# Retention, routed attention and a token mixer on one core: retention outputs ahead of the next scores, weights ahead of the third chunk, token tiles between transposes and outputs of the last batch

## The chip, the cores and the metric

The kernel runs on one core of a Trainium2 chip. Five engines run their own instruction streams and meet at semaphores: TensorE (PE; its weight loads are listed as PEld), VectorE (DVE), ScalarE (ACT), GpSimd (POOL) and SyncE (SP), which here only issues DMAs. The metric is the device time of one execution in microseconds (us). The kernel before takes 981.37 us as the median of 3 runs (979.86 to 984.8).

## The reference, cut to what matters

Three blocks follow each other on 8 batches of 576 positions.

```python
# 1 retention, 8 heads of 64
scores = q @ k.T / 8 ;  x = (scores * gamma_h ** (i - j) * (i >= j)) @ v
# 2 four softmax heads, of which a gate keeps two per position
for e in range(4):
    a = softmax(causal((x @ wq[e]) @ (x @ wk[e]).T / 8))
    out += gate[:, :, e] * (a @ (x @ wv[e]) @ wo[e])
# 3 token mixer on x = out
theta = x @ w_theta
y = w_tok_r @ (x * cos(theta)) + w_tok_i @ (x * sin(theta))
u = x + y ;  out = u + max(u @ w_ch, 0)
```

The weights of block 3 arrive as 64-bit floats, and the kernel itself converts them to pairs of 32-bit numbers.

## The kernel before, in words

The positions of a batch are cut into five chunks of 128 (the last has 64). Numbers are kept as a rounded high part and a rest, so most products are three matmuls (`mm3`, L94 to L96: high by high, low by high, high by low).

**Retention** of a batch is five chunks. `ret_scores` (L132) makes the scores of a chunk in two PSUM tiles named `w`; DVE masks them into `sm` (L137, L140). `ret_out` carries the state in PSUM (`pS`, L153; ACT copies it, L155), makes the output in a third `w` tile (L160 state by queries, L164 `sm` by values), and DVE scales it (`xt`, L171). `ret_step(b, c)` does the scores of chunk c, then the output of chunk c-1. There are three buffers `w`, and they go round: retention, projections (`proj_qk` makes U or KN from x, L94 to L96; `proj_v` makes V and the gate's logits, L225) and later the token tiles take them in turn, so a tile waits until the one three places before it has been read.

**Attention** is 80 units (batch b, head pair p, row tile m), ten per batch. In step t the loop makes the scores of unit t in PSUM tiles `a` (L286; DVE takes the row minimum, L289; ACT the exponential, L294), does what the table `SLOTS` puts there ("Q01 K10" are projections, "R2" is a retention step, capitals of this batch, small letters of the next), transposes the unit before (L333; the copies out of PSUM to `PT` are L338 and L340, one head on DVE, one on ACT), and where a group of row tiles is full makes its outputs (L352, copied by ACT at L356). So retention of batch b+1 and its projections run inside the steps of batch b. PE executes in the order in which this loop is written; the other engines' orders and SP's are made by the framework's scheduler.

**Converting** the weights of block 3 is 53 jobs, dealt out over the steps by `JOBS`: 40 up to step 63, 13 up to step 81. A job is a DMA (`raw`, L413), five DVE operations (L420 to L426), two of ACT and three of POOL, and a DMA back to DRAM.

**The last batch** (steps 70 to 80) has no retention. At step 69 `fuse_load` fetches w_theta and wo; at steps 72 and 73 `fuse` multiplies them (24 matmuls of 512 columns in all). At step 73 `load_o` fetches the attention outputs `ol` and the gates `og` of batches 0 and 1 and POOL multiplies them (L496). `EARLY_AT` sets nine `token_tile`s (1, 1, 2, 2, 1, 2 in steps 75 to 80) behind each step's outputs: 12 matmuls each, six into a `w` tile (x) and six into the single `pS` (theta); ACT copies x (L520), DVE reduces the angle (`k`, L523; `nr`, L525). After the loop `z_tile` (sine and cosine, L606 to L611, then a split to `zh` and `zl`, L99 and L100) feeds `mix` (L665), and `channel` ends the batch.

**The start** (`for c in range(NCH + 1)`): retention of batch 0, with the splits of the four weight tiles `wst` into WH and WL (L99, L100) and the first projections between the chunks. The DMA order there is: chunks 0 and 1, `g0`, one weight tile, chunk 2, three weight tiles.

Of the kernel before, what the change touches and what calls it, by code (L numbers as in the profile page):

```python
# [22 lines left out]
NCH = 5  # L23
# [24 lines left out]
WB = 3  # L48
JOBS = (63, 81)

EARLY_AT = {-5: 1, -4: 1, -3: 2, -2: 2, -1: 1, 0: 2}
EARLY = sum(EARLY_AT.values())

# [4 lines left out]
def tile_kernel(ctx: ExitStack, tc: tile.TileContext, qk, kv, w1, wo, wot, wd, cst, out):  # L58
# [11 lines left out]
    GD = [dram.tile([2, 2, 640], F32, name=f"gd{b}") for b in range(B)]  # L70
    att = pool("att", side="right")
    w1p = pool("w1p", side="right")
    ret = pool("ret", side="right")
# [104 lines left out]

    def ret_step(b, c):
        if c < NCH:  # L180
            ret_scores(b, c)
        if c:
            ret_out(b, c - 1)

# [3 lines left out]
    def proj_qk(b, p, t, g):  # L188
        xh, xl = XT[b]
        if (b, p) not in QKP:  # L190
            QKP[b, p] = (att.tile([128, 2, S], F32R, name="U", bufs=2), att.tile([128, 2, 2, S], F32R, name="KK", bufs=2),
                         att.tile([128, 2, S], F32R, name="KN", bufs=2))
        U, KK, KN = QKP[b, p]
# [62 lines left out]
    def work(b, names):  # L256
        for n in names.split():
            x = b + n.islower()
            if x < B:
                if n in "Gg":  # L260
                    gate(x)
                elif n[0] in "Vv":
# [122 lines left out]
    nc.sync.dma_start(g0, cst[:, o + 1088 + E * E:].rearrange("p (a t) -> p a t", a=4))  # L385
    for c in range(NCH):
# [102 lines left out]
    def load_o(b):  # L489
        OL[b] = wk1.tile([128, 2, S], F32, name="ol", bufs=3)  # L490
        nc.sync.dma_start(OL[b], OD[b])
        gw = wk1.tile([128, 2, S], F32, name="og", bufs=1)
        for s in range(2):
            for p in range(2):
                nc.sync.dma_start(gw[s * 64:s * 64 + 64, p, :], GD[b][p, s, :S].partition_broadcast(64))
        nc.gpsimd.tensor_mul(OL[b], OL[b], gw)  # L496

    def token_tile(pp, g, i):
# [27 lines left out]
        X2[g, i], NR[g, i] = x2, nr  # L526

    units = [(b, p, m) for b in range(B) for p in range(2) for m in range(NCH)]
    nu = len(units)
# [6 lines left out]
    due = [(JOBS[0] - 2) / njobs[0], (JOBS[1] - JOBS[0]) / njobs[1]]  # L536
    early = 0
    outs = []
    for t in range(nu + 1):
        b, k = divmod(t, 10)  # L540
        more, after = SLOTS[k] if t < nu else ("", "")
        if t < nu:
            at_scores(units[t])
            work(b, more)
            if units[t][2] == NCH - 1:
                at_norm(*units[t][:2])
        if t:
# [18 lines left out]
        if t == nu - 11:  # L566
            assert not jobs[0]
            ret.release()
            w2 = pool("w2")
            WOH, WOL, MH, ML = [w2.tile([128, 2, DM], F32R, name=x) for x in ("WOH", "WOL", "MH", "ML")]  # L570
            wa = pool("wa")
            fuse_load()
        if t in (nu - 8, nu - 7):
            fuse(t - nu + 8)
        if t == nu - 7:
            w1p.release()
            wa.release()
            w2b = pool("w2b")
            TK = w2b.tile([128, 9, 2, S], F32R, name="TK")
            wk1 = pool("wk1")  # L580
            load_o(0)
            load_o(1)
            for kt in KORD:
                nc.sync.dma_start(TK[:, kt].bitcast(F32), TD[kt])
        for _ in range(EARLY_AT.get(t - nu, 0)):
            token_tile(ps1, 0, early)
            early += 1
    assert not jobs[1]
# [9 lines left out]
    ps2 = pool("ps2", space=PSUM)  # L598
    ZT = {}

    def z_tile(g, i, h):

        x2, nr = X2[g, i], NR[g, i]
        ds = slice(h * 256, h * 256 + 256)
        cs = wk.tile([128, 2, 256], F32, name="cs", bufs=2)
        nc.vector.tensor_scalar(cs[:, 0, :].bitcast(I32), nr[:, ds].bitcast(I32), 0x7FFFFFFF, None, op0=OP.bitwise_and)  # L606
        nc.vector.tensor_scalar(cs[:, 0, :], cs[:, 0, :], math.pi / 2.0, None, op0=OP.subtract)  # L607
        nc.vector.tensor_scalar(cs[:, 1, :], nr[:, ds], PI_LO, -PI_LO, op0=OP.min, op1=OP.max)
        nc.scalar.activation(cs, cs, AF.Sin)  # L609
        z = cs  # L610
        nc.vector.scalar_tensor_tensor(z, cs, -1.0, x2[:, None, ds].to_broadcast([128, 2, 256]), op0=OP.mult, op1=OP.mult)  # L611
        if i != 4:
            zh = wk.tile([128, 2, 256], F32R, name="zh", bufs=4)
            zl = wk.tile([128, 2, 256], F32R, name="zl", bufs=4)
            split(zh, zl, z)
            ZT[g, i, h] = (zh, zl)
            return
        ZT[g, i, h] = []
        for b in range(2):
            zh = wk.tile([128, 256], F32R, name="zth", bufs=4)  # L620
            zl = wk.tile([128, 256], F32R, name="ztl", bufs=4)
            for a in range(2):
                split(zh[a * 64:a * 64 + 64], zl[a * 64:a * 64 + 64], z[b * 64:b * 64 + 64, a, :])
            ZT[g, i, h].append((zh, zl))

    UT = {}
# [72 lines left out]

    for i in range(early, 5):  # L700
        token_tile(ps2, 0, i)
    for b in range(B):
        q = [x for x in nxt_tiles(b) if x[0] or x[1] >= early]
        if b % 2 and b + 1 < B:
# [10 lines left out]
    ps2.release()  # L715
    wk.release()
    wk1.release()
    w2b.release()
    w2.release()
    cvt.release()  # L720
# [78 lines left out]
```

## Time and profile before

| | us |
|---|---|
| median of 3 runs | 981.37 |
| the profiled execution, its own time | 983.44 |
| its span, first to last instruction | 981.7 |
| PE busy in the span | 930.5 |
| DVE busy | 648.9 |
| ACT busy | 442.7 |
| POOL busy | 244.3 |

The span is what the rows below divide up; the execution's own time is 1.74 us longer, and it lies 2.07 us above the median. "Idle before" and what ended it is given in square brackets in a timeline. The granted clock of PE stands as a share of full speed: 1.00 is 2.4 GHz, 0.50 is 1.2 GHz, and values between are a mean over a stretch.

### The profile page before, as it was taken

The numbers are of one execution on the slowest core, as the hardware profiler recorded it, in microseconds if no ns is written. First come the engines' busy times: TensorE is split into PE (matmuls) and PEld (weight loads), VectorE is DVE, ScalarE is ACT, GpSimd is POOL, SyncE is SP. The second block draws the span as 40 slices with busy tenths as digits, with TensorE's granted clock in tenths as the row PEclk, the third lists the DMA queues.
The fourth block names the chain that finished last, engine by engine and source line by source line (L and its number), as shares of the span: only waits on it lengthen the run. The fifth ranks groups of instructions, "written<-read, shape, count | busy, mean of one in ns | idle before, by whom it ended". The sixth has DMA issues, their size and how long they took to land.

```text
span 981.7 us, 21532 instructions
## 1 busy us (share of the span) xinstructions
PE 930.5 (95%) x8090; PEld 854.7 (87%) x8090; DVE 648.9 (66%) x1843; ACT 442.7 (45%) x1198; POOL 244.3 (25%) x290
## 2 busy tenths in 40 slices
PE   6999999999999899998977799999999999999998
PEld 5989888888898889887755799999999999999998
DVE  4477767768776787776557974495656846486533
ACT  2355546555564565555544533333343432344320
POOL 4324243342524334142214111021201102020110
PEclk9999999999999999999989999999999999999999
DMA  9856647556666566636755300021101001010001
GB/s 265 227 144 204 177 156 191 172 170 191 189 181 192 149 185 211 158 108 178 219 223 166 133 24 26 26 73 49 49 2 37 37 1 49 1 49 2 25 26 49
DMA packets 81016, 115.69 MB, mean 118 GB/s; under 512 B 17680, under 2 KB 55952, under 8 KB 80912
## 3 DMA queue, kind: packets, MB, share of 16 engines
q1 hardware_dynamic: 80768, 114.03, 39.0%
q8 instruction: 64, 1.05, 0.5%
q0 software_dynamic: 144, 0.28, 0.1%
q14 instruction: 40, 0.33, 0.1%
HBM read 71.94 MB, written 23.74 MB: 97 GB/s over the span
## 4 chain that ended last, share of the span: by engine, by line
PE 72%; DVE 12%; DMA 5%; ACT 5%; issue 2%; SPq 2%; POOL 1%; ACTq 0%; DVEq 0%; POOLq 0%
PE acc L665 22%; PE w L94 8%; PE w L95 8%; PE w L96 8%; PE a L286 4%; PE w L225 4%; PE a L352 4%; PE w L132 3%; PE w L164 3%; PE a L333 2%; PE w L160 2%; DMA raw<-wd 2%; DVE P L289 2%; PE acc L655 2%; DVE U L211 2%
## 5 line engine op out<-in xcount | busy, mean ns | idle before, releaser
L665 PE MATMUL acc<-TK,zh 128*128 128x256 f32 (+1 forms) x1024 | 185.0, 303 | 3.9 <-ACT zh L99 3.9
L665 PEld LDWEIGHTS acc<-TK,zh 128*128 128x128 f32 x1024 | 153.4, 191 | 4.8 <-ACT zh L99 4.3
L294 ACT ACTIVATE P<-P,st 128x128 f32<-128x128 f32 (+4 forms) x160 | 95.5, 598 | 55.6 <-DVE st L289 54.9
L665 PE MATMUL acc<-TK,zl 128*128 128x256 f32 (+1 forms) x512 | 110.8, 298 | 0.0
L691 POOL TENSOR_TENSOR o<-o,ul 128x576 f32<-128x576 f32 x28 | 42.5, 1522 | 229.8 <-DVE o L686 186.6
L289 DVE CUSTOM_DVE_ANT_0 P<-a,cm 128x128 f32<-128x128 f32 (+4 forms) x160 | 72.1, 478 | 27.7 <-PE a L286 27.4
L665 PEld LDWEIGHTS acc<-TK,zl 128*128 128x128 f32 x512 | 86.8, 190 | 0.1
L609 ACT ACTIVATE cs<-cs 128x512 f32<-128x512 f32 x72 | 45.3, 630 | 90.4 <-DVE cs L607 86.3
L611 DVE SCALAR_TENSOR_TENSOR cs<-cs,x 128x512 f32<-128x512 f32 x72 | 61.3, 856 | 26.7 <-ACT cs L609 26.3
L286 PE MATMUL a<-KK,U 128*64 128x288 f32 (+4 forms) x384 | 77.1, 329 | 1.3 <-issue 0.9
L94 PE MATMUL w<-uh,CH 128*128 128x256 f32 (+1 forms) x256 | 76.0, 298 | 2.4 <-DVE nr L525 1.3
L94 PE MATMUL w<-xh,WH 128*128 128x288 f32 x256 | 76.3, 298 | 0.0
L99 ACT ACTIVATE zh<-cs 128x512 fp32r<-128x512 f32 x64 | 40.2, 629 | 80.0 <-PE acc L665 61.1
L96 PE MATMUL w<-xh,WL 128*128 128x288 f32 x256 | 76.0, 297 | 0.0
L95 PE MATMUL w<-xl,WH 128*128 128x288 f32 x256 | 75.9, 296 | 0.0
L95 PE MATMUL w<-ul,CH 128*128 128x256 f32 (+1 forms) x256 | 75.7, 296 | 0.0
L100 DVE TENSOR_TENSOR zl<-cs,zh 128x512 fp32r<-128x512 f32 x64 | 45.2, 710 | 46.2 <-ACT zh L99 45.4
L96 PE MATMUL w<-uh,CH 128*128 128x256 f32 (+1 forms) x256 | 75.7, 296 | 0.0
L429 POOL TENSOR_TENSOR r<-r,ex 128x192 f32<-128x192 f32 (+1 forms) x51 | 29.3, 575 | 185.4 <-ACT hl L430 93.6
L352 PE MATMUL a<-PT,V 128*64 128x192 f32 (+3 forms) x576 | 57.1, 320 | 11.4 <-DVE PT L338 7.7
L286 PEld LDWEIGHTS a<-KK,U 128*128 128x128 f32 (+1 forms) x384 | 53.7, 172 | 12.5 <-issue 5.6
L100 DVE TENSOR_TENSOR ul<-acc,uh 128x256 fp32r<-128x256 f32 x64 | 25.7, 451 | 58.4 <-ACT uh L99 58.1
(141 smaller groups left out, 2266.3 us busy)
## 6 DMA issues: line engine op xcount, KB each, us to landing
kv<-kv SPq DMA_DIRECT2D x40, 512.0 KB
KK<-KN SPq DMA_DIRECT2D x128, 144.0 KB
raw<-wd SPq DMA_DIRECT2D x43, 192.0 KB
qz<-qk SPq DMA_DIRECT2D x64, 128.0 KB
kt<-qk SPq DMA_DIRECT2D x32, 256.0 KB
out<-o SPq DMA_DIRECT2D x28, 288.0 KB
td<-hl SPq DMA_DIRECT2D x27, 192.0 KB
TK<-td SPq DMA_DIRECT2D x9, 576.0 KB
```

The source lines that it names most:

```text
L94: nc.tensor.matmul(ps, ah, bh, start=first, stop=False)
L95: nc.tensor.matmul(ps, ah, bl, start=False, stop=False)
L96: nc.tensor.matmul(ps, al, bh, start=False, stop=last)
L100: nc.vector.tensor_sub(l, src, h)
L286: nc.tensor.matmul(ps[s][:R], U[:, s, rs], KK[:, s, x, j0:j1], start=x == 0, stop=x == 1)
L289: MARK["dve"] = nc.vector.tensor_tensor_reduce(Ps[s][:R, j0:j1], ps[s][:R], cm[:R, o + j0:o + j1], 1.0, st[:R, 0, s:s + 1] if i else 3.0e3 ...
L294: MARK["act"] = nc.scalar.activation(Ps[s][:R, :n], Ps[s][:R, :n], AF.Exp, bias=st[:R, last, s:s + 1], scale=-1.0, accum_out=SUM[p][:R, m, ...
L352: nc.tensor.matmul(po[s * 64:s * 64 + 64, c0:], V[:ROWS[j], j, 2 * p + s, :], v, start=j == 0, stop=j == last, skip_group_check=True)
L609: nc.scalar.activation(cs, cs, AF.Sin)
L611: nc.vector.scalar_tensor_tensor(z, cs, -1.0, x2[:, None, ds].to_broadcast([128, 2, 256]), op0=OP.mult, op1=OP.mult)
L665: nc.tensor.matmul(acc[d][j], A[:, dc], TK[:, kt, W, t0:t1], start=q == 0 and n == 0, stop=q == 8 and n == 2)
L691: nc.gpsimd.tensor_add(o, o, ul[:, et, :].bitcast(F32))
```

## The change

Four edits. First, `ret_step` makes the output of chunk c-1 before the scores of chunk c. Second, the four weight tiles are fetched ahead of chunk 2 of batch 0, and the start is written out: scores 0 and 1, output 0, output 1, two V projections, and then scores and output of chunks 2, 3 and 4 directly behind each other; the scale `gt` is made chunk by chunk. Third, a table `LAST` replaces `SLOTS` and `EARLY_AT` in the last batch: each step has work before the transposes, between transposes and outputs, and after; the two `fuse` products and the nine token tiles ("T") stand there, theta of every second tile goes to a `w` buffer, `load_o` of batches 0 and 1 moves from step 73 to 69, and the first two z tiles are made before the loop's buffers are given back (their pool `zp` takes the place of U, KK and KN, which have a pool of their own now). Fourth, `JOBS` is (58, 75): conversions end six steps earlier.

```diff
-JOBS = (63, 81)
-EARLY_AT = {-5: 1, -4: 1, -3: 2, -2: 2, -1: 1, 0: 2}
+JOBS = (58, 75)
+EARLY = 9
+LAST = [("Q01", "K10", ""), ("K11", "", ""), ("Q10", "F0", ""), ("Q11", "F1", ""), ("", "T", ""),
+        ("T", "T", ""), ("T", "", ""), ("T", "", ""), ("T", "T", ""), ("", "T", ""), ("", "T", "")]
...
     def ret_step(b, c):
+        if c:
+            ret_out(b, c - 1)
         if c < NCH:
             ret_scores(b, c)
-        if c:
-            ret_out(b, c - 1)
...
-    load_w1(0)
+    for kt in range(4):
+        load_w1(kt)
     for c in range(2, LDB):
         loads(0, c)
-    for kt in range(1, 4):
-        load_w1(kt)
...
-    for c in range(NCH + 1):
-        ret_step(0, c)
-        if c < 4:
-            split_w1(c)
-        work(-1, ("", "", "", "v0", "v1 k00", "v2 q00")[c])
+    ret_scores(0, 0)
+    make_gt(0)
+    ret_scores(0, 1)
+    ret_out(0, 0)
+    make_gt(1)
+    for kt in range(4):
+        split_w1(kt)
+        if kt == 1:
+            ret_out(0, 1)
+    for c in range(2, NCH):
+        make_gt(c)
     w1s.release()
-    work(-1, "v3 k01 v4 g")
+    work(-1, "v0 v1")
+    for c in range(2, NCH):
+        ret_scores(0, c)
+        ret_out(0, c)
+        work(-1, ("", "v2 k00", "q00 v3 k01 v4 g")[c - 2])
...
         if pp is ps1:
-            th = pp.tile([128, 4, 128], F32, name="pS", bufs=1).rearrange("p a d -> p (a d)")
+            if i % 2:
+                th = pp.tile([128, DM], F32, name="w", bufs=WB)
+            else:
+                th = pp.tile([128, 4, 128], F32, name="pS", bufs=1).rearrange("p a d -> p (a d)")
...
-        if after or b >= B - 1:
-            work(b, after)
+        work(b, between)
+        if between or b == B - 1:
             for o in outs:
                 at_out(*o)
             outs = []
+        work(b, after)
...
             fuse_load()
-        if t in (nu - 8, nu - 7):
-            fuse(t - nu + 8)
+            load_o(0)
+            load_o(1)
...
-            load_o(0)
-            load_o(1)
...
+    for i in range(2):
+        z_tile(0, i, 0)
```

How it moves PE at a retention step (step 15: the scores of chunk 4 and the output of chunk 3 of batch 2; the projection k00 ends just ahead). Before:

```order
L333 MATMUL a<-ident,P 128x128 x4
L132 MATMUL w<-qz_121,kt 64x2x64 x4
L153 MATMUL pS<-vp,kv 64x64 x8
L160 MATMUL w<-qz_123,S_120 64x128 x8
L164 MATMUL w<-sm_124,vp 64x128 x2
L164 MATMUL w<-sm_125,vp 64x128 x2
```

and after (the same calls stand some lines lower):

```order
L341 MATMUL a<-ident,P 128x128 x4
L157 MATMUL pS<-vp,kv 64x64 x8
L164 MATMUL w<-qz_126,S_123 64x128 x8
L168 MATMUL w<-sm_127,vp 64x128 x2
L168 MATMUL w<-sm_128,vp 64x128 x2
L136 MATMUL w<-qz_124,kt 64x2x64 x4
```

The scores (`kt`) went from ahead of the state to behind the output, and with them the turn in which the three `w` buffers are taken.

PE in step 78 of the last batch, where a group's outputs (`V`) follow the transposes (`P`). Before:

```order
L286 MATMUL a<-KK,U 128x512 x4
L333 MATMUL a<-ident,P 128x128 x6
L352 MATMUL a<-PT,V 64x256 x4
L352 MATMUL a<-PT,V 64x128 x2
L94 MATMUL w<-WOH,oh 128x512
```

and after:

```order
L341 MATMUL a<-ident,P 128x128 x6
L98 MATMUL w<-WOH,oh 128x512
L99 MATMUL w<-WOL,oh 128x512
...
L99 MATMUL pS<-ML,oh 128x512
L100 MATMUL pS<-MH,oll 128x512
L360 MATMUL a<-PT,V 64x256 x4
L360 MATMUL a<-PT,V 64x128 x2
L294 MATMUL a<-KK,U 64x288 x8
```

A whole token tile (12 matmuls) came between the transposes and the outputs that read their copies.

SP's queue about steps 71 to 74: `KK` are the keys of the last head pair, needed by the scores of step 75; `wost` is wo, `ol` and `og` belong to `load_o`. Before:

```order
L458 DMA wost<-wo 128x256
L358 DMA od_66<-ob 128x576
L440 DMA cd_78<-hl 256x1x192
L203 DMA KK<-KN 64x2x288 x4
L413 DMA raw<-wd 128x384
L440 DMA cd_78<-hl 256x1x128
L491 DMA ol<-od_60 128x1152
L495 DMA og<-gd_85 64x576 x4
```

and after:

```order
L466 DMA wost<-wo 128x256
L513 DMA og<-gd_85 64x576
L509 DMA ol<-od_61 128x1152
L207 DMA KK<-KN 64x2x288 x2
L513 DMA og<-gd_86 64x576 x4
L207 DMA KK<-KN 64x2x288 x2
L366 DMA od_66<-ob 128x576
L207 DMA KK<-KN 64x2x288 x4
```

The loads of `ol` and `og` went ahead of the last keys, half of which now stand behind a gate load of batch 1.

## Rows read from the trace of the kernel before

**Rows 1.** The page, busy time of PE and the others over the span

```profile
PE 930.5 (95%) x8090; PEld 854.7 (87%) x8090; DVE 648.9 (66%) x1843; ACT 442.7 (45%) x1198; POOL 244.3 (25%) x290
```

**Rows 2.** Stretches: length, busy (count) by engine, PE clock, DMA share, GB/s

```profile
31.00:450.00 419.00, 403.51 (x4413) 364.00 (x4408) 308.70 (x1043) 231.40 (x741) 154.61 (x205) 1.00 0.61 174
450.00:544.00 94.00, 73.52 (x412) 57.60 (x411) 56.56 (x176) 48.56 (x133) 22.74 (x26) 0.93 0.65 211
544.00:564.00 20.00, 18.89 (x126) 18.06 (x127) 19.03 (x47) 10.93 (x22) 2.72 (x1) 0.91 0.26 80
```

**Rows 3.** PE's waits over the span: us in total, times, longest

```profile
PE a L352 <- DVE PT L338: 7.7, 6, 3.3
PE w L160 <- DVE KN L100: 5.7, 3, 2.7
PE w L160 <- ACT lg L229: 3.8, 3, 1.8
PE w L164 <- DVE U L211: 3.1, 7, 0.7
```

**Rows 4.** Timeline of PE at two retention steps: start, length, what

```profile
115.87 1.52 PE L132 MATMUL w<-qz,kt 128*64 128x256 f32 x16
117.22 0.63 PE L153 MATMUL pS<-vp,kv 128*64 128x64 f32 x16
118.60 1.09 PE L164 MATMUL w<-sm,vp 128*64 128x128 f32 x16 [0.75 <-DVE U L211]
...
321.68 1.09 PE L160 MATMUL w<-qz,S 128*64 128x128 f32 x16 [2.67 <-DVE KN L100]
```

**Rows 5.** Timeline of DVE ahead of the wait that ended at 321.68

```profile
319.35 0.26 DVE L420 TENSOR_SCALAR b<-raw 128x192 int32<-128x192 int32 x1 [3.14 <-DMA raw<-wd]
321.16 0.46 DVE L100 TENSOR_TENSOR KN<-w,KN 128x288 fp32r<-128x288 f32 x1
```

**Rows 6.** Timeline of PE in the first 31 us

```profile
16.24 2.96 PE L132 MATMUL w<-qz,kt 128*64 128x256 f32 x14 [3.20 <-DMA kt<-qk]
...
23.96 1.52 PE L132 MATMUL w<-qz,kt 128*64 128x256 f32 x16 [2.16 <-DMA kt<-qk]
...
27.62 0.74 PE L225 MATMUL w<-WH,xh 128*128 128x260 f32 x4
...
29.24 0.66 PE L132 MATMUL w<-qz,kt 128*64 128x128 f32 x8
```

**Rows 7.** Timeline of ACT in the first 31 us

```profile
20.36 2.35 ACT L99 ACTIVATE WH<-wst 128x772 fp32r<-128x772 f32 x3
```

**Rows 8.** Timeline of PE in the last batch and behind it

```profile
462.24 0.43 PE L352 MATMUL a<-PT,V 128*64 128x128 f32 x2 [1.55 <-ACT PT L338]
...
466.50 0.33 PE L94 MATMUL w<-xh,WH 128*128 128x288 f32 x1
...
494.41 0.70 PE L352 MATMUL a<-PT,V 128*64 128x128 f32 x4 [3.27 <-DVE PT L338]
...
498.19 0.63 PE L95 MATMUL pS<-ML,oh 128*128 128x512 f32 x1
...
513.03 0.50 PE L94 MATMUL w<-WOH,oh 128*128 128x512 f32 x1
...
515.88 0.39 PE L94 MATMUL w<-WOH,oh 128*128 128x512 f32 x1
...
543.90 0.89 PE L665 MATMUL acc<-TK,zh 128*128 128x256 f32 x5 [3.88 <-ACT zh L99]
```

**Rows 9.** Timeline of ACT, POOL and DVE in the last batch

```profile
461.13 0.42 ACT L99 ACTIVATE wt<-wost 128x256 fp32r<-128x256 f32 x1 [0.84 <-DMA wost<-wot]
...
461.94 0.24 ACT L338 COPY PT<-a 128x128 f32<-128x128 f32 x1
...
526.46 2.72 POOL L496 TENSOR_TENSOR ol<-ol,og 128x1152 f32<-128x1152 f32 x1 [0.78 <-DMA og<-gd]
...
526.59 2.63 DVE L302 TENSOR_SCALAR nw<-sum 128x10 f32<-128x10 f32 x1
```

More of the change, by code (lines that the diff above doesn't have):

```diff
@@ L71, in tile_kernel @@
     att = pool("att", side="right")
+    atk = pool("atk", side="right")
     w1p = pool("w1p", side="right")
@@ L190, in proj_qk @@
         if (b, p) not in QKP:
-            QKP[b, p] = (att.tile([128, 2, S], F32R, name="U", bufs=2), att.tile([128, 2, 2, S], F32R, name="KK", bufs=2),
-                         att.tile([128, 2, S], F32R, name="KN", bufs=2))
+            QKP[b, p] = (atk.tile([128, 2, S], F32R, name="U", bufs=2), atk.tile([128, 2, 2, S], F32R, name="KK", bufs=2),
+                         atk.tile([128, 2, S], F32R, name="KN", bufs=2))
         U, KK, KN = QKP[b, p]
@@ L261, in work @@
                     gate(x)
+                elif n[0] == "T":
+                    token_tile(ps1, 0, len(X2))
+                elif n[0] == "F":
+                    fuse(int(n[1]))
                 elif n[0] in "Vv":
@@ L385, in tile_kernel, with make_gt @@
     nc.sync.dma_start(g0, cst[:, o + 1088 + E * E:].rearrange("p (a t) -> p a t", a=4))
-    for c in range(NCH):
+    def make_gt(c):
         R = ROWS[c]
@@ L476, in fuse @@
         split(MH[:, p, :], ML[:, p, :], acc)
-    for c in range(NCH + 1):
-        ret_step(0, c)
-        if c < 4:
-            split_w1(c)
-        work(-1, ("", "", "", "v0", "v1 k00", "v2 q00")[c])
-    w1s.release()
-    work(-1, "v3 k01 v4 g")
+    ret_scores(0, 0)
[9 more added lines that the diff above has]
+        make_gt(c)
+    w1s.release()
+    work(-1, "v0 v1")
[3 more added lines that the diff above has]
+        work(-1, ("", "v2 k00", "q00 v3 k01 v4 g")[c - 2])
     X2, NR, OL = {}, {}, {}
     def load_o(b):
-        OL[b] = wk1.tile([128, 2, S], F32, name="ol", bufs=3)
+        OL[b] = wol.tile([128, 2, S], F32, name="ol", bufs=3)
         nc.sync.dma_start(OL[b], OD[b])
-        gw = wk1.tile([128, 2, S], F32, name="og", bufs=1)
+        gw = wol.tile([128, 2, S], F32, name="og", bufs=1)
         for s in range(2):
@@ L526, in token_tile, with z_tile @@
         X2[g, i], NR[g, i] = x2, nr
+    ZT = {}
+    def z_tile(g, i, h):
+        if (g, i, h) in ZT:
+            return
+        x2, nr = X2[g, i], NR[g, i]
+        ds = slice(h * 256, h * 256 + 256)
+        cs = zp.tile([128, 2, 256], F32, name="cs", bufs=2)
+        nc.vector.tensor_scalar(cs[:, 0, :].bitcast(I32), nr[:, ds].bitcast(I32), 0x7FFFFFFF, None, op0=OP.bitwise_and)
+        nc.vector.tensor_scalar(cs[:, 0, :], cs[:, 0, :], math.pi / 2.0, None, op0=OP.subtract)
+        nc.vector.tensor_scalar(cs[:, 1, :], nr[:, ds], PI_LO, -PI_LO, op0=OP.min, op1=OP.max)
+        nc.scalar.activation(cs, cs, AF.Sin)
+        z = cs
+        nc.vector.scalar_tensor_tensor(z, cs, -1.0, x2[:, None, ds].to_broadcast([128, 2, 256]), op0=OP.mult, op1=OP.mult)
+        if i != 4:
+            zh = zp.tile([128, 2, 256], F32R, name="zh", bufs=4)
+            zl = zp.tile([128, 2, 256], F32R, name="zl", bufs=4)
+            split(zh, zl, z)
+            ZT[g, i, h] = (zh, zl)
+            return
+        ZT[g, i, h] = []
+        for b in range(2):
+            zh = zp.tile([128, 256], F32R, name="zth", bufs=4)
+            zl = zp.tile([128, 256], F32R, name="ztl", bufs=4)
+            for a in range(2):
+                split(zh[a * 64:a * 64 + 64], zl[a * 64:a * 64 + 64], z[b * 64:b * 64 + 64, a, :])
+            ZT[g, i, h].append((zh, zl))
     units = [(b, p, m) for b in range(B) for p in range(2) for m in range(NCH)]
@@ L536, in tile_kernel @@
     due = [(JOBS[0] - 2) / njobs[0], (JOBS[1] - JOBS[0]) / njobs[1]]
-    early = 0
     outs = []
@@ L540, in tile_kernel @@
         b, k = divmod(t, 10)
-        more, after = SLOTS[k] if t < nu else ("", "")
+        if b < B - 1:
+            more, between, after = *SLOTS[k], ""
+        else:
+            b = B - 1
+            more, between, after = LAST[t - 10 * b]
         if t < nu:
@@ L546, in tile_kernel @@
                 at_norm(*units[t][:2])
+        if t == nu - 1:
+            atk.release()
+            zp = pool("zp")
         if t:
@@ L570, in tile_kernel @@
             WOH, WOL, MH, ML = [w2.tile([128, 2, DM], F32R, name=x) for x in ("WOH", "WOL", "MH", "ML")]
+            wol = pool("wol")
             wa = pool("wa")
             fuse_load()
-        if t in (nu - 8, nu - 7):
-            fuse(t - nu + 8)
+            load_o(0)
+            load_o(1)
         if t == nu - 7:
@@ L580, in tile_kernel @@
             wk1 = pool("wk1")
-            load_o(0)
-            load_o(1)
             for kt in KORD:
                 nc.sync.dma_start(TK[:, kt].bitcast(F32), TD[kt])
-        for _ in range(EARLY_AT.get(t - nu, 0)):
-            token_tile(ps1, 0, early)
-            early += 1
+    for i in range(2):
+        z_tile(0, i, 0)
     assert not jobs[1]
@@ L598, in tile_kernel @@
     ps2 = pool("ps2", space=PSUM)
[L599 to L624, printed above, removed]
     UT = {}
@@ L698, in nxt_tiles @@
         return [(g + 1, i) for i in range(5)] if b + 1 < B else []
-    for i in range(early, 5):
-        token_tile(ps2, 0, i)
     for b in range(B):
-        q = [x for x in nxt_tiles(b) if x[0] or x[1] >= early]
+        q = [x for x in nxt_tiles(b) if x not in X2]
         if b % 2 and b + 1 < B:
@@ L716, in tile_kernel @@
     wk.release()
+    zp.release()
     wk1.release()
     w2b.release()
+    wol.release()
     w2.release()
```

1 line of the change is left out of this document (removed).

## The prediction

> **What bounds the kernel now.** I read the busy line first: PE has 930.5 us of work in a span of 981.7 us, DVE 648.9 [rows 1]. PE is the bound, so only three things can move the time: PE's idle time, PE's time at the slower clock, and PE's work, which the change leaves at the same instructions. The table by stretches then says where the idle time lies [rows 2]: 419 − 403.51 = 15.5 us in the 419 us of retention and attention at full clock; 94 − 73.52 = 20.5 us in the 94 us of the last batch, at a clock of 0.93; 20 − 18.89 = 1.1 us in the next 20 us at 0.91. The rest of the 51 us lies in the start and at the end. The table of PE's waits names the releasers [rows 3], and the timelines show the places [rows 4 to 9]. The profiled execution is 983.44 us, its span 981.7; the sum is made on it, and 2.07 us are taken off at the end to stand at the median of 981.37.
>
> **The swap of output and scores.** The waits of retention that it can touch are L160 on KN (5.7 us, 3 times), L160 on the logits (3.8, 3) and L164 on U (3.1, 7): 12.6 us [rows 3]. None is a wait for data. `w` has three buffers in turn, and each of these instructions takes the one of a projection that DVE or ACT has not read yet. Before, the order behind a projection is scores tile 1, scores tile 2 (1.52 us together), state (0.63), L160, L164 [rows 4]. After, it is state, L160, L164, scores 1, scores 2. So the third user of a buffer after the projection's end comes at another distance. On R1 (the L164 wait) the output's tile takes the free buffer and the scores take those of the projection about 0.5 us earlier than L164 asked for its buffer before: seven waits grow by 0.5, +3.5. On R3 the tile that waited for the logits is asked for about 0.45 later, 3 × 0.45 = −1.35. On R4, whose waits reach 2.67 us [rows 4], the buffer of the last KN is asked for some 1.3 us later, behind an L160 and L164 of 1.09 and 1.04: 3 × 1.3 = −3.9. Together −1.75. The bounds are all 12.6 gone, and the seven waits one us longer, +7; I take −1.7 because the long waits are not made by the order on PE at all. The one at 321.68 began on DVE, which stood 3.14 us at the head of its queue for the `raw` of a conversion, with the KN subtraction behind it [rows 5]. A shift of 1.3 us takes a part of that and no more.
>
> **The conversions.** 40 jobs by step 58 instead of 63 put one job in every 1.4 steps instead of 1.525, 9% denser. Each brings a `raw` DMA that DVE can stand behind, as above. A ninth more of the 5.7 + 3.8 us of such waits is +0.9; bounds 0 and three more waits of 2.67, +8. In return fewer jobs are left in the last batch, whose DVE is freer for copies; that stands in the tail's sum.
>
> **The start.** Two DMA waits of 3.20 and 2.16 us ahead of L132 [rows 6] are waits for chunks 1 and 2. With the weights ahead of chunk 2 the second is covered by the V projections, and the first partly by other work. But all of WH must then be split before the first V projection, where before one split stood behind each chunk: ACT's three splits took 2.35 us from 20.36 on [rows 7], and PE reached its first projection at 27.62 [rows 6]. I place the end of the splits at about 20.3, a new wait of some 4 us behind output 1; and scores, mask and output of one chunk now stand directly behind each other, three times about 0.7 us. Going through the first 44 us instruction by instruction with the durations of these rows gives −0.7. Bounds: both DMA waits go and nothing comes, −5.4; the 4 us and 2.1 us come and only 3.2 go, +3.
>
> **The last batch.** What could be recovered: 20.5 idle (the 1.1 behind it I leave out, the change touches nothing there), and the slow clock: (1 − 0.93) × 94 = 6.6 and (1 − 0.91) × 20 = 1.8 [rows 2]. That is 28.9 us. The pattern is in the timeline [rows 8]: transposes, then outputs that wait for the copies (1.55, 3.27), and behind such a wait the same matmul of 512 columns takes 0.63 instead of 0.39, so a wait is paid twice. After, a token tile, six matmuls into `w` and six of theta, stands between; from 513.03 to the next tile at 515.88 is 2.85 us, more than a PT copy and its wait of 1.55 and a little less than the longest of 3.27 [rows 8]. With every second theta in `w` no tile waits for the one before it to be reduced. The wait of 3.88 for `zh` at the start of `mix` [rows 8] goes because two z tiles are made before the loop's buffers are given back. What stays, each by its row: steps 71 and 76 have no tile between transposes and outputs, and in step 71 the copy to PT stands on ACT behind a split of wo that waits for its DMA (461.13, copy at 461.94) [rows 9]: 2 × 1.55 = 3.1. One slow stretch behind it, as from 462.24 to 466.50 [rows 8] at half the rate, 4.3 / 2 = 2.1. POOL's multiplies of `ol` (2.72 us each): DVE's operation on 128x10 took 2.63 us beside one [rows 9], and I put 1.5 of it on the path. 0.6 at the start of `mix`, and an eighth of the 20.5 for small releases of `a`, 2.5. Sum 9.8, so the gain is 28.9 − 9.8 = 19.1. Bounds: 28.9, and −7 where only the `zh` wait and the wait of 3.27 go.
>
> The row of DVE beside POOL is what the page SBUF — State Buffer of the Trainium skill describes in its section "Who interferes with whom": whichever of VectorE and GpSimd starts first on the shared port pair holds it for its whole instruction, and the other is fully blocked; the 2.63 us inside 2.72 agree [rows 9]. By that rule alone, with the three multiplies all on the path, 3 × 2.7 = 8.1 us instead of 1.5 would be lost, and the tail would give 12.5.
>
> **Sum.** −1.7 + 0.9 − 0.7 − 19.1 = −20.6. The profiled execution would be 962.8 with a span near 961.1; less 2.07 that is 960.8, and I write 961.
>
> **Rivals.** (1) The tail opens wholly: every tile covers every copy and PE never slows, −28.9 − 1.5 = −30.4, 951. For it: 2.85 us of cover is more than five of the six waits that make up the 7.7 us of L352 [rows 3]; against it: two steps have no cover. Chance 0.12.
>
> (2) The waits come back one stage earlier. `load_o` now stands at step 69, and SP's queue has gate loads between halves of the last keys; the single `og` must be multiplied by POOL (2.72 us, [rows 9]) before batch 1 can be loaded into it, and keys behind that load reach the scores of step 75 late. One wait of 2.7 for keys, and one DVE lock like that of 494.41 with its slow stretch (3.27 and as much again at half rate, 6.6) give 9.3 back: −11.3, 970. For it: the order of SP; against it: three to four steps of projections lie in between. The rule of the port named above makes for this case too. Chance 0.19.
>
> (3) Slower: the swap makes every retention step behind a projection wait. If each of the 14 outputs behind a projection (two in each of seven batches) waits the 2.67 of the longest today [rows 4] and seven R3 scores wait the mean of 3.8 / 3 = 1.3 [rows 3], that is 46 us in place of 12.6, +34; with the tail's −19.1, and the other two terms, +15: 996. It decides from retention waits of about 36 us on, where the time is 0.5% above today. For it: second scores now take a buffer just written by L164; against it: before, only 13 waits came of 35 steps, with the same three buffers. Chance 0.06.
>
> (4) The change does not do what it says: the outputs of a group wait as long, because the copies are late for DVE's own reasons (its queue, not PE's distance), and the token tiles' angles queue on DVE ahead of the PT copies. Then little but the 3.88 of `zh` is won and retention takes it back: 980. Chance 0.05.
>
> **How the numbers follow.** Forecast 0.58, and the four rivals 0.12, 0.19, 0.06, 0.05. About 5 us, 0.5%, is what a measurement of this kernel can tell from no change. Faster: 0.58 + 0.12 + 0.19 = 0.89; same 0.05; slower 0.06. The forecast's own range is 955 to 967 (a third of the tail's remainder either way and the two bounds of the start). Eight times in ten: from 951, the first rival, to 974, past the second; that leaves out the third, the fourth and the lower half of the first.
>
> **What the changed profile would show.** The tail: PE's idle in the last batch about 7 us and the clock near 0.97; waits for `PT` below 4 us in all; no wait of L98 for `nr`; the first `mix` matmul without a wait above 1. Wrong if PE waits for KK near step 75, or if DVE shows operations of 2.6 us beside L496's successor that PE waits for. Retention: the waits of L160 and L164 give way to waits of the scores for U, KN and logits, about 11 us in sum; wrong if the sum passes 20. Start: no wait for kt above 1 us after the first chunk, one of about 4 us ahead of the first V projection, and the first attention scores 0.7 earlier than before. Wrong in the whole if the stretch of retention is longer by more than the last batch is shorter.

## The result, and the profile after

The changed kernel takes 958.45 us (median of 4 runs, 955.35 to 960.74) against 981.11 us of the kernel before: ratio 0.9749, 95% interval 0.9716 to 0.9781. Forecast were 961 us, 951 to 974, and "faster" at 0.89. The profiled execution is 958.07 us with a span of 956.3. The two profiles lie 25.4 us apart in their spans and the medians 22.7, because the profiled execution of the kernel before lay 2.3 above its median.

The page's first line says where to look: PE has 5.5 us less busy time than in [rows 1], with the same matmuls, and the span is 25.4 us shorter. So most of the gain is idle time; the rest is matmuls that no longer run at half rate, as the table below shows for the last batch (PE's busy time 72.72 before, 64.16 after, at a clock of 0.93 and 1.00).

```profile
PE 925.0 (97%) x8090; PEld 854.3 (89%) x8090; DVE 643.0 (67%) x1843; ACT 441.0 (46%) x1198; POOL 247.8 (26%) x290
```

I cut both traces at the same instructions: the first attention scores, the first scores of step 70, and the first matmul of `mix`. Before, as a table by stretches (length, busy time and count of PE, PEld, DVE, ACT, POOL, then PE clock, DMA share, GB/s):

```profile
43.88:450.70 406.82, 391.33 (x4284) 352.23 (x4283) 306.09 (x1037) 227.36 (x729) 149.63 (x199) 1.00 0.61 173
450.70:543.90 93.20, 72.72 (x406) 56.80 (x404) 56.12 (x175) 48.56 (x133) 22.31 (x25) 0.93 0.65 209
543.90:981.70 437.80, 431.32 (x2980) 412.82 (x2980) 267.40 (x595) 154.51 (x310) 53.22 (x32) 1.00 0.10 33
```

and after:

```profile
45.39:446.01 400.62, 391.62 (x4285) 356.40 (x4283) 303.89 (x1057) 228.21 (x737) 156.21 (x212) 1.00 0.63 179
446.01:514.43 68.42, 64.16 (x405) 51.22 (x404) 50.33 (x156) 45.68 (x125) 13.12 (x12) 1.00 0.69 217
514.43:956.30 441.87, 432.11 (x2980) 413.65 (x2980) 268.29 (x594) 154.81 (x310) 56.61 (x33) 0.99 0.12 41
```

Four differences make the 25.4 us. The start is 45.39 − 43.88 = 1.5 longer; the middle 406.82 − 400.62 = 6.2 shorter; the last batch 93.20 − 68.42 = 24.8 shorter, at a clock of 1.00 instead of 0.93; and the mixer 441.87 − 437.80 = 4.1 longer. The last one was in no term of my sum.

PE's waits after (line, what it waited for, us in total, times, longest):

```profile
PE w L136 <- DVE U L215: 7.3, 8, 1.6
PE w L229 <- DVE WL L104: 2.7, 2, 1.4
PE w L98 <- ACT uh L103: 2.6, 1, 2.6
PE w L136 <- DMA kt<-qk: 2.6, 1, 2.6
PE acc L693 <- DVE ul L104: 2.4, 1, 2.4
PE w L229 <- ACT WH L103: 1.6, 3, 0.7
PE acc L693 <- ACT zh L103: 1.3, 1, 1.3
...
PE a L360 <- DVE PT L346: 0.6, 2, 0.4
```

Against [rows 3] the waits of the outputs for `PT` went from 7.7 to 0.6 us and those of retention for KN and logits are gone but for one of 0.4. In their place stand waits for U (7.3), for the weight splits (2.7 and 1.6), and three around the start of the mixer: `zh` 1.3, which ends where the mixer begins, `uh` 2.6 and `ul` 2.4.

### The profile page after: what moved, and what is told of

Same layout as the page of the kernel before. It is cut to its first block, busy times and chain, and to the rows that moved or that the text cites. A ratio compares the mean times of both kernels' runs of the same rounds, so it can differ in the third digit from the quotient of the medians.

```text
span 956.3 us, 21524 instructions
## 1 busy us (share of the span) xinstructions
PE 925.0 (97%) x8090; PEld 854.3 (89%) x8090; DVE 643.0 (67%) x1843; ACT 441.0 (46%) x1198; POOL 247.8 (26%) x290
## 4 chain that ended last, share of the span: by engine, by line
PE 79%; DVE 9%; ACT 5%; DMA 3%; issue 2%; SPq 1%; POOL 1%; DVEq 0%; ACTq 0%; POOLq 0%
PE acc L693 24%; PE w L98 8%; PE w L99 8%; PE w L100 8%; PE w L229 6%; PE a L294 5%; PE w L136 5%; PE a L360 4%; PE a L341 3%; PE w L164 3%; PE w L168 3%; PE acc L683 2%; ACT P L302 2%; PE pS L157 1%; DVE U L215 1%
## 5 line engine op out<-in xcount | busy, mean ns | idle before, releaser
L297 DVE CUSTOM_DVE_ANT_0 P<-a,cm 128x128 f32<-128x128 f32 (+4 forms) x160 | 72.1, 477 | 14.8 <-PE a L294 14.2
L98 PE MATMUL w<-uh,CH 128*128 128x256 f32 (+1 forms) x256 | 76.0, 298 | 3.3 <-ACT uh L103 2.6
L563 DVE SCALAR_TENSOR_TENSOR cs<-cs,x 128x512 f32<-128x512 f32 x72 | 62.0, 868 | 25.0 <-ACT cs L561 24.8
L98 PE MATMUL w<-xh,WH 128*128 128x288 f32 x256 | 76.0, 297 | 0.0
L136 PE MATMUL w<-qz,kt 128*64 128x128 f32 (+1 forms) x576 | 57.5, 323 | 9.8 <-DVE U L215 7.3
```

Of the source, the lines that this page charges most:

```text
L98: nc.tensor.matmul(ps, ah, bh, start=first, stop=False)
L136: nc.tensor.matmul(ps[e][g, i, :, j * 64:R], t[:, hp, j * 64:j * 64 + 64], qz[:, :, hp, j * 64:R], start=True, stop=True, skip_group_check ...
L297: MARK["dve"] = nc.vector.tensor_tensor_reduce(Ps[s][:R, j0:j1], ps[s][:R], cm[:R, o + j0:o + j1], 1.0, st[:R, 0, s:s + 1] if i else 3.0e3 ...
```

## What gave time back in the mixer

The timelines of DVE and POOL in the changed kernel, around the start of the mixer (start, length, what; x4 and x2 are operations run one behind the other):

```profile
506.31 2.67 DVE L310 TENSOR_SCALAR nw<-sum 128x10 f32<-128x10 f32 x1
...
521.60 4.28 DVE L104 TENSOR_TENSOR ztl<-cs,zth 64x256 fp32r<-64x256 f32 x4
...
532.08 3.72 DVE L563 SCALAR_TENSOR_TENSOR cs<-cs,x 128x512 f32<-128x512 f32 x2
535.73 1.54 DVE L104 TENSOR_TENSOR ul<-acc,uh 128x256 fp32r<-128x256 f32 x4
```

```profile
506.29 2.65 POOL L514 TENSOR_TENSOR ol<-ol,og 128x1152 f32<-128x1152 f32 x1 [17.49 <-DMA og<-gd]
521.27 2.98 POOL L514 TENSOR_TENSOR ol<-ol,og 128x1152 f32<-128x1152 f32 x1 [12.33 <-DMA og<-gd]
532.40 2.86 POOL L514 TENSOR_TENSOR ol<-ol,og 128x1152 f32<-128x1152 f32 x1 [8.15 <-DMA og<-gd]
```

and PE in the same stretch:

```profile
514.43 0.77 PE L693 MATMUL acc<-TK,zh 128*128 128x256 f32 x4 [1.28 <-ACT zh L103]
515.04 0.43 PE L693 MATMUL acc<-TK,zl 128*128 128x256 f32 x2
...
532.99 0.86 PE L98 MATMUL w<-uh,CH 128*128 128x256 f32 x3 [2.57 <-ACT uh L103]
536.29 0.77 PE L693 MATMUL acc<-TK,zh 128*128 128x256 f32 x2 [2.45 <-DVE ul L104]
...
538.08 0.63 PE L693 MATMUL acc<-TK,zh 128*128 128x256 f32 x2
```

Each POOL multiply has DVE operations beside it that are longer by most of the multiply's length: 2.67 us for one on ten columns, 4.28 for four that take 1.76 elsewhere (537.79), and 3.72 for two that take 1.30. These are the gates of batches 2, 3 and 4, while PE starts the first token tile of batch 2 only at 582.54; each starts when its gate load lands (what ended POOL's idle time in brackets), so the scheduler sets them as early as their data allow. The one at 532.40 stands between PE and `ul`, and behind that wait two matmuls of 256 columns take 0.63 us, where two take 0.43 at 515.04. The kernel before had the same multiplies, the one at 538.63 in the time in which PE waited for `zh` anyway. The run late_mul tests it.

## The experiments

Each kernel was timed in 5 rounds against the kernel before on the same chip, in three sets of four; the medians of the kernel before were 981.18, 981.55 and 982.55 us in them. Differences in us against the changed kernel compare medians across these sets. "Middle", "last batch" and "mixer" are the three stretches above, from one profiled execution each. The seven kernels with the swap and JOBS = (58, 75) differ in no edit of the middle, and yet it is 400.1 to 404.8 us in their profiles; so a difference of the middle below 5 us needs more than one pair of profiles.

**swap_only.** The kernel before with one edit; the start calls `ret_step` too, so its order changes with it.

```diff
+        if c:
+            ret_out(b, c - 1)
         if c < NCH:
             ret_scores(b, c)
-        if c:
-            ret_out(b, c - 1)
```

> The kernel before with ret_step in the new order (output of chunk c-1, then scores of chunk c) and nothing else. The two traces put 406.8 us between the first attention scores and step 70 before and 400.6 after. Theory A (the swap made this, by the turn of the w buffers): waits of L160 for KN and logits (9.5 us) go to under 1, the scores take over the waits for U, about 6 us in place of 3.1; the stretch falls by 5 to 6 us, the time by the same. Rival B (my sum on record): -1.7 us in the stretch. Rival C (the conversions, not the swap, made it): under 1 us. Last batch as before within 2 us in each case.

974.99 us, ratio 0.9927 (0.9901 to 0.9954). Its first two stretches, and DVE at the place that answers to [rows 5]:

```profile
44.37:440.99 396.62, 391.44 (x4284) 356.63 (x4283) 298.08 (x1037) 226.50 (x729) 149.58 (x200) 1.00 0.62 177
440.99:536.08 95.09, 74.07 (x405) 57.22 (x404) 59.83 (x175) 48.45 (x133) 22.09 (x25) 0.91 0.66 209
```

```profile
310.85 0.62 DVE L420 TENSOR_SCALAR b<-raw 128x192 int32<-128x192 int32 x1 [0.52 <-DMA raw<-wd]
...
313.03 0.46 DVE L100 TENSOR_TENSOR KN<-w,KN 128x288 fp32r<-128x288 f32 x1
```

The middle fell by 10.2 us, to within 5.2 of PE's busy time. Theory A, and more than it said: the waits for KN and logits are gone, and DVE waited for `raw` 3.6 us in the middle instead of 10.8. Rivals B and C are out: without the swap the middle is 404.6 to 407.9 in three profiles, with it and the first 40 conversions as before 396.6 to 397.8 in four. By median only 6.2 us are left, because the last batch is 1.9 longer, the start 0.5, and the profile of the kernel before lay above its median.

The DMA behind the DVE wait for `raw` in [rows 5] and behind the one shown here, in SP's queue (SPq), by the turn of the two `raw` buffers (of the x2 the first); the kernel before comes first:

```profile
313.28 0.91 SPq L413 DMA_DIRECT2D raw<-wd  x2
```

```profile
305.25 1.50 SPq L413 DMA_DIRECT2D raw<-wd  x1
```

DVE was free for it at 316.21 and at 310.34. So SP issued it 2.9 us ahead of that in the kernel before and 5.1 us ahead in swap_only; DVE read it 6.1 and 5.6 us after its issue.

**tail_only.** The changed kernel without the swap, the new start and the new JOBS.

```diff
-JOBS = (58, 75)
+JOBS = (63, 81)
...
         if c < NCH:
             ret_scores(b, c)
+        if c:
+            ret_out(b, c - 1)
```

> The changed kernel with the start, ret_step and JOBS of before: only the table LAST, the earlier load_o, the early z tiles and the pools are new. Theory A (the tiles between transposes and outputs make the tail's gain, whatever else): step 70 to the first mix matmul falls from 93.2 to 68 to 70 us, the mixer takes 4 us longer as in the changed kernel, time 20 to 21 below before. Rival B (the earlier end of the conversions made a good part of it, by freeing DVE in the last steps): with 13 jobs up to step 81 the waits of L360 and L341 come back in steps 75 to 80, the stretch is 75 to 82, time 9 to 14 below before.

966.86 us, ratio 0.9853 (0.9826 to 0.988). Middle 404.6, last batch 73.8, mixer 439.6. By time it is 14.3 below before, between the two theories. The table LAST with the moved loads and z tiles takes 19.4 us from the last batch; 5.4 of the 24.8 are missing, and the wait of `mix` for `zh` is 6.4 us instead of 1.3:

```profile
522.13 1.81 PE L683 MATMUL acc<-TK,zh 128*128 128x256 f32 x6 [6.41 <-ACT zh L103]
```

The next run shows that the earlier end of the conversions is what is missing, about a fifth of the gain there.

**old_jobs.** The changed kernel with one line as before.

```diff
-JOBS = (58, 75)
+JOBS = (63, 81)
```

> The changed kernel with JOBS = (63, 81), conversions as thin as before. Theory A (denser conversions make DVE late for the minima that hold up ACT's copy of U): the three waits of L136 for U of 1.4 to 1.6 us fall to 0.4, the stretch from the first attention scores to step 70 falls by 3.5 us; the last batch has more jobs and gets 2 to 6 us longer; time within 3 of the changed kernel. Rival B (jobs have nothing to do with these waits): the stretch stays at 400.6 within 1 us. Rival C (jobs are free in the last batch too): step 70 to mix stays at 68.4 within 1 us.

961.93 us, ratio 0.9801 (0.9777 to 0.9825):

```profile
44.87:442.18 397.31, 391.57 (x4284) 356.59 (x4283) 299.72 (x1037) 226.69 (x729) 149.34 (x200) 1.00 0.62 177
442.18:516.04 73.86, 64.29 (x406) 51.31 (x404) 53.56 (x173) 46.79 (x130) 16.84 (x22) 0.98 0.68 218
```

Theory A in both halves: with thinner conversions the middle is 3.3 us shorter and the waits for U fall from 7.3 to 4.0 us, none over 0.8; the last batch is 5.4 longer. The denser conversions cost 3.3 and bring 5.4, and another 1.5 in the mixer. By time the interval just touches that of the changed kernel. How a wait for U grows, at the same place of both kernels (DVE's row minima of a step, the changed kernel first):

```profile
174.76 0.69 DVE L297 CUSTOM_DVE_ANT_0 P<-a,cm 128x512 f32<-128x512 f32 x1
```

```profile
173.64 0.69 DVE L297 CUSTOM_DVE_ANT_0 P<-a,cm 128x512 f32<-128x512 f32 x1
```

In the changed kernel a conversion's operations stand ahead of these minima; ACT's copy of U follows the exponentials, at 176.92 against 175.80, and PE waits 1.61 us for U instead of 0.41. In the last batch 4.4 of the 5.4 us are the wait for `zh`:

```profile
516.04 1.81 PE L693 MATMUL acc<-TK,zh 128*128 128x256 f32 x6 [5.66 <-ACT zh L103]
```

This run has the two early z tiles and their pool, as tail_only has, and still waits longer for `zh` than the kernel before (3.88). So it is the end of the conversions at step 75 that makes this wait short.

**old_start.** The changed kernel with the start of before (the diff above read backwards).

```diff
-    for kt in range(4):
-        load_w1(kt)
+    load_w1(0)
     for c in range(2, LDB):
         loads(0, c)
+    for kt in range(1, 4):
+        load_w1(kt)
```

> The changed kernel with the start of before (weights behind chunk 2, scores and outputs of batch 0 in the old order). The first attention scores came at 43.88 before and 45.39 after. Theory A (the new start costs by its waits for the weight splits, 4.3 us, and matmuls at half rate behind them): first scores at 43.9 again, time 1.5 below the changed kernel, ratio to before about 0.973. Rival B (what the start loses it gives back in batch 1, whose first stretch waits for the loads of retention): same time as the changed kernel within 0.5 us. Rival C (my prediction: the new start is the faster by 0.7): 0.7 above the changed kernel.

954.99 us, ratio 0.9733 (0.9707 to 0.9759), which overlaps with the changed kernel's. In its profile the first scores come at 45.92, later than in the changed kernel, while its median is lower; the profiled execution, 958.65, was the slowest of its six. One profile of a start that waits for loads does not decide this; late_old_start repeats it.

**late_mul.** The changed kernel, the gates' multiplies of batches 2 to 7 bound behind POOL's last add.

```diff
-        nc.gpsimd.tensor_mul(OL[b], OL[b], gw)
+        if b < 2:
+            nc.gpsimd.tensor_mul(OL[b], OL[b], gw)
+        else:
+            with tc.issue_after(MARK["add"].ins):
+                nc.gpsimd.tensor_mul(OL[b], OL[b], gw)
...
-            nc.gpsimd.tensor_add(o, o, ul[:, et, :].bitcast(F32))
+            MARK["add"] = nc.gpsimd.tensor_add(o, o, ul[:, et, :].bitcast(F32))
```

> The changed kernel, but POOL multiplies ol by og for batches 2 to 7 only behind the adds (L719) of the batch before, two at a time; the loads stay where they are. In the changed kernel three of these multiplies run at 506.3, 521.3 and 532.4, and DVE operations beside them take 2.67, 4.28 (four) and 3.72 us (two). Theory A (they lock DVE, and that gives back what the tail had won: zh late by 1.28, uh by 2.57, ul by 2.45, then PE at half rate): step 70 to mix falls from 68.4 to about 67, mix to the end from 441.9 to 437.5 to 439, no DVE operation near 3 us in the first 40 us of the mixer; time 4 to 6 below the changed kernel. Rival B (the first mix stretch is short of DVE time anyway, 34 of 40 us busy, because PE arrives with only two z tiles ready): the waits for uh and ul shrink by under 1 us each, time within 1.5 of the changed kernel. Rival C (the multiplies now come too late for the token tiles of the next batches): new waits of L98 for oh, time above.

950.04 us, ratio 0.9674 (0.9649 to 0.97), 8.4 below the changed kernel:

```profile
447.25:514.78 67.53, 64.14 (x406) 51.26 (x404) 48.22 (x156) 44.80 (x123) 10.35 (x11) 1.00 0.73 230
514.78:948.80 434.02, 429.13 (x2980) 411.23 (x2980) 263.32 (x594) 155.31 (x312) 57.83 (x34) 1.00 0.12 40
```

PE's waits from 505 to 560 us are down to two:

```profile
PE w L98 <- ACT uh L103: 0.8, 1, 0.8
PE acc L697 <- ACT ob L364: 0.6, 1, 0.6
```

The DVE operations that had stood beside the multiplies, here without one:

```profile
507.32 0.17 DVE L310 TENSOR_SCALAR nw<-sum 128x10 f32<-128x10 f32 x1
...
521.72 1.77 DVE L104 TENSOR_TENSOR ztl<-cs,zth 64x256 fp32r<-64x256 f32 x4
...
529.83 1.30 DVE L567 SCALAR_TENSOR_TENSOR cs<-cs,x 128x512 f32<-128x512 f32 x2 [0.15 <-ACT cs L565]
```

and the first 40 us of the mixer, the changed kernel first:

```profile
514.43:554.43 40.00, 34.98 (x239) 33.95 (x240) 34.25 (x78) 19.36 (x37) 5.84 (x2) 0.91 0.38 132
```

```profile
514.78:554.78 40.00, 39.18 (x290) 38.28 (x291) 33.02 (x86) 20.58 (x40) 1.44 (x1) 1.00 0.20 73
```

Theory A, with a larger size: the mixer is 7.85 us shorter, not 3 to 4.5. 4.9 of it is idle time of PE and 3.0 is busy time, as the first 40 us stay at clock 1.00 instead of 0.91. Of the three operations 2.50, 2.51 and 2.42 us went; the last two lie in the mixer, and DVE is busy for 5.0 us less there, so that is the time for which it had stood blocked. That agrees with the page SBUF — State Buffer of the Trainium skill ("Who interferes with whom"), by which the blocked engine stands still for the other's whole instruction.

**tiles_behind.** The changed kernel, the tiles that stand between transposes and outputs put behind the outputs.

```diff
-... ("", "T", ""), ("T", "T", ""), ("T", "", ""), ("T", "", ""), ("T", "T", ""), ("", "T", ""), ("", "T", "")]
+... ("", "", "T"), ("T", "", "T"), ("T", "", ""), ("T", "", ""), ("T", "", "T"), ("", "", "T"), ("", "", "T")]
```

> The changed kernel with the token tiles that stand between transposes and outputs put behind the outputs; of the steps with outputs this concerns 75, 78 and 80. Theory A (the cover of 2.85 us is what removed the waits for PT): three waits of L360 for PT of 1.2 to 3 us come back with slow clock behind them, step 70 to mix 74 to 79 instead of 68.4, time 5 to 9 above the changed kernel. Rival B (the waits went for other reasons: second theta buffer, earlier multiplies, fewer conversions, so DVE copies in time): waits for PT under 1.5 us in all, stretch within 2 us of 68.4.

962.37 us, ratio 0.9791 (0.9765 to 0.9817), 3.9 above the changed kernel, though the two intervals overlap; last batch 71.98, clock 1.00 there. Waits of PE in it:

```profile
PE a L360 <- DVE PT L346: 2.6, 5, 1.1
```

Between the two: three short waits come back beside the two that the changed kernel has (0.6 us), none long, and PE's wait at the start of `mix` grows from 1.28 to 2.35. Of the 24.8 us the place of the tiles holds 3.6, not the greater part.

**theta_pS.** The changed kernel, theta always in `pS`.

```diff
-            if i % 2:
+            if False:
                 th = pp.tile([128, DM], F32, name="w", bufs=WB)
```

> The changed kernel with theta of every token tile in pS as before. Theory A (the single buffer made a wait of 0.7 to 1.0 us per pair of tiles): waits of L98 for nr of 3 to 5 us in the last batch, 1.5 to 2 us at half rate behind them, stretch 72 to 75 instead of 68.4. Rival B (steps lie far enough apart now, since work stands between any two tiles): 68.4 within 1 us; only the two tiles of steps 75 and 78 would wait, under 1 us each.

963.72 us, ratio 0.9788 (0.9759 to 0.9818). Last batch 71.08, 2.7 longer; four waits of L98 for `nr` before `mix`, 3.0 us in all, where the changed kernel has none. That is theory A at the lower end of its waits, with a stretch somewhat shorter than its 72 to 75. Its first scores came at 47.15 in the profile and its interval overlaps with the changed kernel's, so not all of the 5.3 us by median is this edit's.

**no_early_z.** The changed kernel without the two calls.

```diff
-    for i in range(2):
-        z_tile(0, i, 0)
```

> The changed kernel without the call that makes two z tiles ahead of the mixer; mix makes them, from the same pool zp. Theory A (the pool in free space is what counts, the scheduler starts them early in either case): mix still starts within 1 us of 68.4 after step 70. Rival B (the place in the code counts): the wait of the first mix matmul for zh grows from 1.3 to 3.5 to 5 us, with a slower clock behind it, time 3 to 5 above the changed kernel.

957.34 us, ratio 0.9742 (0.9717 to 0.9766), as the changed kernel; last batch 67.28, the wait for `zh` 1.1 us. Theory A in that the calls' place is worth nothing. That the pool in memory that is free early lets the scheduler start the tiles is not shown: no run takes the pool back.

**late_before.** The kernel before with the edit of late_mul.

> The kernel before with the multiplies of ol for batches 2 to 7 put behind the adds of the batch before, as in the run late_mul, where the mixer took 434.0 us instead of 441.9. In the kernel before such multiplies run at 526.5, 538.6 and 549.1, and the mixer takes 437.8. Theory A (434 is a mixer without locked DVE; the kernel before paid 3.8 of it too, and the 4.1 that the change gave back are its bigger share of the same cost): mixer 434 to 435, time 3 to 5 below before, plus 0 to 2 in the last batch. Rival B (the cost is new: it comes from DVE being short when mix starts earlier, and the kernel before does not pay it): mixer 437 to 438, time same as before within 1.5.

978.96 us, ratio 0.9954 (0.9934 to 0.9975). Mixer 435.6 instead of 437.8, last batch 91.7 instead of 93.2: theory A by time, while the mixer lies between the 434 to 435 of A and the 437 to 438 of B. So the kernel before already paid some 3.7 us for these multiplies, and the changed kernel 8.4. In the mixer alone it is 2.2 before and 7.85 after, a difference that more than covers the 4.1 that the change gave back there.

**late_old_start, late_jobs, late_both.** late_mul with the start of before; with JOBS = (63, 75); with both.

```diff
-JOBS = (58, 75)
+JOBS = (63, 75)
```

> The run late_mul (950.0) with the start of before. First attention scores in the profiles so far: 43.8 to 44.4 in three kernels with the old DMA order, but 45.9 in old_start; 44.9 to 47.2 in six with the new one. Theory A (the new start costs 1 to 2.5 us): 948 to 949, first scores at about 44 to 45. Rival B (starts scatter with the loads, and the two are alike): 950 within 0.7.

947.01 us, ratio 0.9623 (0.9596 to 0.9651), 3.0 below late_mul; first scores at 43.56 instead of 46.59. Theory A, slightly more than its range.

> The run late_mul with JOBS = (63, 75): the first 40 conversions as thin as before, the other 13 in 12 steps instead of 17. Theory A (density of the first 40 costs 3.3 us in the stretch up to step 70, as old_jobs showed, and in the last batch only jobs behind step 75 hurt): first scores to step 70 397.3, step 70 to mix 67 to 69, time 3 to 4 below late_mul, 946 to 947. Rival B (any denser jobs in the last steps make DVE late there): step 70 to mix 71 to 74, time as late_mul or above.

946.27 us, ratio 0.9618 (0.9592 to 0.9644), 3.8 below late_mul. Middle 397.8, last batch 69.0, mixer 433.6: theory A, with 1.5 us lost in the last batch.

> late_mul with both the start of before and JOBS = (63, 75). If both theories A hold their gains add: 944 to 946. If neither does: 950 within 1. If only the jobs do: 946 to 947.

943.66 us, ratio 0.9593 (0.9567 to 0.962), 14.8 below the changed kernel and the fastest of all:

```profile
44.07:440.84 396.77, 391.51 (x4285) 356.53 (x4283) 298.69 (x1047) 227.19 (x733) 151.88 (x205) 1.00 0.63 179
440.84:511.15 70.31, 65.19 (x405) 52.60 (x403) 49.07 (x163) 45.67 (x126) 13.95 (x17) 0.98 0.68 213
511.15:944.60 433.45, 429.26 (x2980) 411.23 (x2980) 264.07 (x597) 156.43 (x313) 57.98 (x34) 1.00 0.12 42
```

The two gains add, to slightly more than the range of 944 to 946: 3.0 + 3.8 = 6.8 by the two runs alone, 6.4 measured.

## Why the prediction was right, step by step

Direction, time and range held: 961 forecast, 958.45 measured. That the sum came within 2.6 us is partly luck: the swap gave some 8 us more than its term, the first stretch of the mixer took back 4.1 that no term had, the conversions cost 3.3 where 0.9 stood and the start about 3 where −0.7 stood.

- **The last batch**, −19.1 forecast. In its own stretch 24.8 went, 16.2 of idle time and 8.6 of PE's busy time, nearly all of the 27.1 that I had called recoverable there, so rival 1 came true in size; behind it 4.1 were given back, net 20.7. The remainder of 9.8 us was mis-sized: for the two uncovered steps I put 3.1, and the outputs of step 71 waited 0.37 + 0.24; the slow stretch of 2.1 did not come. I had put 1.5 us for POOL's multiplies and placed them in the batch; they came as waits for `uh` and `ul` behind it, with the slow clock, and late_mul puts them at 8.4. The 8.1 that the prediction names beside the 1.5 was nearer. I also ascribed the gain too much to the tiles in between: undoing that alone costs 3.6 us in the stretch, a single theta buffer 2.7, the conversions 5.4. The wait for `zh` fell from 3.88 to 1.28, but not by the two z tiles made early, as I had it: without these calls it is 1.12, and with them but with conversions to step 81 it is 5.66. For some 13 of the 24.8 us no run undoes an edit. One candidate is the move of `load_o`: in the kernel before, the multiply at 489.61 made DVE's split for a token tile last 1.84 us (the same split takes 0.41 to 0.43 elsewhere), ahead of the row minima and the copy behind the wait of 3.27 at 494.41 [rows 8]:

```profile
490.69 1.84 DVE L100 TENSOR_TENSOR oll<-ol,oh 128x256 fp32r<-128x256 f32 x1 [3.81 <-PE a L286]
```

  After, the same pair falls at 475.35 and 476.43, and no wait for `PT` follows within 12 us. How much of the 13 us this is stays open.
- **The swap**, −1.7 forecast, −10.2 measured alone in the middle (7 to 11 by the other profiles, see swap_only). Two steps failed. "Seven waits grow by 0.5" did not happen: alone, the seven R1 waits for U are 0.38 to 0.76, 3.1 us in all as in [rows 3], and an eighth of 0.73 comes at the first units. I had counted the second scores tile from the wrong end; its buffer is taken after state, output and the first tile, nearly as late as L164 took it before. And "a shift of 1.3 us takes a part of that and no more" was wrong for KN and logits: all 9.5 us went. The shift is one part of it. The other is that DVE's wait for `raw` ahead of KN was 0.52 us in swap_only and 3.14 in [rows 5], since SP issued that DMA 2.2 us earlier against DVE's work. That the output, now ahead of the scores, frees the buffers for the retention loads that stand before it in SP's queue sooner would explain this; it is argued and not shown. The two parts are not separated by any run.
- **The conversions**, +0.9 forecast inside bounds of 0 to 8 (9% of 9.5 us; the "ninth" in the text would be 1.06): 3.3 in the middle, between 2.3 and 8.2 by the eleven profiles with either JOBS, as three waits for U of 1.4 to 1.6 us in place of 0.4. The way was not the one I named. DVE did not stand at `raw` before KN; its conversion work delayed the row minima, ACT's exponentials then held up ACT's copy of U, and PE waited for that. In the last batch and mixer they brought 6.9, which the forecast left to the tail's sum without a size.
- **The start**, −0.7 forecast, about +3 by the medians (3.0 for late_mul against late_old_start, 2.6 for late_jobs against late_both), +1.5 by the mean of the seven profiles with either order of the loads. The wait for the splits came as forecast, 2.7 + 1.6 = 4.3 us where I had put some 4. What failed was "the first partly by other work": a DMA wait of 2.57 ahead of the second scores stayed, and V's matmuls behind the splits ran at half rate:

```profile
10.16 1.50 PE L136 MATMUL w<-qz,kt 128*64 128x256 f32 x15 [2.57 <-DMA kt<-qk]
...
21.91 0.58 PE L229 MATMUL w<-WL,xh 128*128 128x260 f32 x1 [1.36 <-DVE WL L104]
...
23.16 1.07 PE L229 MATMUL w<-WH,xh 128*128 128x260 f32 x4
...
34.28 0.63 PE L229 MATMUL w<-WL,xh 128*128 128x260 f32 x4
```

Four matmuls take 1.07 us at 23.16 and 0.63 at 34.28. I had worked the start out at the full clock.

- **Rivals.** Rival 2 (keys late behind the gate loads, a locked DVE) gave 0.56 us for the keys; its second half came true in another place. Rivals 3 and 4 did not occur.
- **The signs.** Two that were named as "wrong if" came although the time held: a wait for KK (0.56), and DVE operations of 2.6 us beside the multiply that PE then waited for. Waits of the outputs for `PT` (0.9 us in all) and PE's idle time in the last batch (4.3) were better than stated; the first `mix` matmul waited 1.28 where at most 1 was stated, a kt wait of 2.57 stayed, and the first attention scores came 1.5 us later instead of 0.7 earlier.

## What to carry to other kernels

Cut both traces at the same instructions and sum the stretches before judging a term; here a sum near the truth hid a swap mis-sized by 8 us and a give-back of 4. When a stall is removed, look at which background work of other engines now falls into the first stretch behind it, and pin work that nobody needs yet behind an instruction of its own engine. A wait for a rotating buffer can go by the order of its users: here one swap with no other edit took 9.5 us of such waits.

## What was not expected of the hardware

A POOL multiply of 2.7 to 3.0 us made the DVE operations beside it 2.4 to 2.5 us longer, as one such row before had shown; moving six of them, three of which stood around the start of the mixer, was worth 8.4 us here and 3.7 in the kernel before. Starts scatter: with the new start the first attention scores came at 44.9 to 47.2 us in seven profiles, with the old DMA order at 43.3 to 45.9 in seven, so a change of one us there needs medians, not a profile.
